# Linear attention, then a top-1 mixture of experts: narrower expert passes, one store fewer at the end, the later decays made earlier, and the stores of places one at a time

## The chip, the cores and the metric

The kernel runs on one core of a Trainium2 chip. The metric is the device time of one execution in microseconds (us), the median over the runs. Lower is better.

## The reference

Two blocks follow each other. Attention works on 4 batches of 8 heads, 768 positions and head size 64, all in fp32, with a decay `lam[h]` per head. In steps of 64 positions (the kernel takes 128):

```python
intra = einsum('bhij,bhjd->bhid', einsum('bhic,bhjc->bhij', qb, kb) * Dmask, vb)  # Dmask[i,j] = lam**(i-j), i >= j
inter = einsum('bhid,bhde->bhie', qb * lam**(pos+1), kv_state)
out[block] = intra + inter
kv_state   = lam**block * kv_state + einsum('bhsd,bhse->bhde', kb * lam**(block-1-pos), vb)
```

The result is laid out as 3072 tokens of 512 numbers. Each token then goes to the one of 8 experts with the highest gate logit:

```python
logits = x @ w_gate                       # 512 -> 8
e      = argmax(logits);  gate = softmax(logits)[e]
out[t] = gate * (relu(x[t] @ w1[e]) @ w2[e])   # 512 -> 1024 -> 512
```

With the reference's own inputs experts 0 to 7 get 385, 361, 364, 401, 418, 380, 356 and 407 tokens.

## The kernel before

**Attention** runs in 12 steps: 6 stretches of 128 positions, each in two steps of two batches. One step turns q and k on TensorE (line 227), scales k for the state on GpSimd (`kd`, line 255), multiplies q with k (`sp`, line 265), applies the decay mask on VectorE (`mt`, line 271), multiplies with v (`op`, line 299), adds the part of the state (`op`, line 290), and makes the state's update (`cp`, line 324). The function `enter(i)` does the loads, the turns and `kd` of step i; it is called one step ahead. Most instructions are pinned with `pin`, so that an engine runs them in the order in which the code writes them. Each engine, and each DMA queue, is a queue in that order.

**Decays.** The mask `decay` and `kdec` are made at the start. `later_decays()` (line 967) makes two more tables on VectorE, `qdec` and `sdec`, by copies and four scans. They are first used in the steps of the second stretch, by `qs_room` (line 241) and `sd` (line 336). Before, they are made after the first step's state has been copied (line 344).

**Places.** When the experts of a group of tokens are known, `ranks` and `put` work out each token's place in its expert's list, and `store(j)` (line 449) writes 128 list entries of 16 bytes to DRAM with an indirect DMA on GpSimd's queue. There are 24 such stores. `store_places()` (line 1018) issues two or three of them back to back at the end of a step, with a small memset between two of them. After the group called `early` is stored, `start_early()` loads the first list of expert 5 and gathers its 256 rows (lines 475 and 505), so that this pass can begin while attention ends.

**Experts.** Expert 5 comes first, in a part of 256 and a part of 128 places. The other seven are sorted on the device by how many tokens they have, and pass i takes `CAPS[i]` places whatever expert it is; unused places hold a row of zeros. Each of these passes has two stages, x times w1 (line 706) and hidden times w2 (line 889), with 112 matmuls each: 7 products instead of 8 are made from halves of the operands, so a matmul is `CAPS[i]/2` columns wide. If a count is beyond its `CAPS[i]`, a loop at the end (after the branches on `beyond`, lines 1270 to 1279) takes the rest in blocks of 128 rows, with the weights loaded again.

**The last pass** (`outputs_fast`, line 810 and after) makes its second stage in tiles of 128 rows. Rows 0 to 255 are made as four quarters. Its inner function `give(i, k, p)` finishes the quarter of row tile i and column half k and stores it at once, as half rows (`scatter_half`, line 527). Rows from 256 on are a tile of their own (`lone_tile`, stored by line 511).

Of the kernel before, what the change touches and what calls it, by code (L numbers as in the profile page):

```python
# [12 lines left out]
I32 = mybir.dt.int32  # L13
# [9 lines left out]
def kernel(  # L23
# [29 lines left out]
    nc = tc.nc  # L53
# [4 lines left out]
    P = 128  # L58
    C = P
    NSTEP = S // C  # L60
# [2 lines left out]
    FC = F // P  # L63

    FIRST = 5
    CAPS = [384, 424, 408, 408, 392, 368, 368, 360]
    TG = 3
    NR = E - 1

# [96 lines left out]
            data1=ident, initial=0.0, op0=ALU.mult, op1=ALU.add)  # L166

    kdec = const.tile([P, H], F32, name="kdec")
    nc.vector.tensor_copy(kdec.rearrange("p (g u) -> p u g", u=2), decay[:, :, :, C - 1])

    so_far = [const.tile([P, E], BF16, name="none_yet")]
    nc.vector.memset(so_far[0], 0.0)
# [45 lines left out]
    def pin(inst):  # L218
        tc.keep_in_program_order(inst)
# [89 lines left out]
    def to_sbuf(m):  # L309
        m.xT = work.tile([P, DC, 2, C], F32, tag="xT", name="xT", bufs=1)  # L310
        first = nc.scalar.copy(m.xT[:, :, 0, :], m.op[0])  # L311
        if swapped(m):
            with tc.issue_after(first.ins):
                nc.scalar.copy(m.xT[:, :, 1, :], m.op[1])
        else:
            for u in range(2):
                nc.scalar.copy(m.xT[halves[u], :, 1, :], m.op[1][halves[1 - u]])

    def grow(m):

# [196 lines left out]

    def half_rows(m):

        m.halves = small.tile([P, 2, 2], I32, tag="half_ids", name="half_ids", bufs=1)  # L520
        for k in range(2):
            pin(nc.vector.tensor_scalar(out=m.halves[:, :, k], in0=m.ids[:, :2, 1], scalar1=2,
                                        scalar2=k, op0=ALU.mult, op1=ALU.add))

    def scatter_half(idx, src):

        put = nc.gpsimd.indirect_dma_start(
            out=out.rearrange("n (k d) -> (n k) d", k=2),
            out_offset=bass.IndirectOffsetOnAxis(ap=idx, axis=0), in_=src,
            in_offset=None, bounds_check=2 * N - 1, oob_is_err=False)  # L530
        tc.declare_no_dep(put.ins, group="rows", reason="a token is on one list, once")
        tc.add_to_no_dep_group("rows", put.ins)
        return put
# [290 lines left out]
    def outputs_fast(m, w2t, b):  # L824
        a, t = left_of(m.hT, 0, P, pair_rooms_of_sums()), m.third
        o, outs, (p1, u2, u3, u4) = pair_rooms()
        add = nc.vector.tensor_add

        def scaled(i, k, u):
            nc.scalar.activation(outs[i][k], u, ACT.Copy, scale=at(m, i)[2])  # L830

        def give(i, k, p):
            pin(nc.vector.scalar_tensor_tensor(
                out=outs[i][k], in0=p, scalar=at(m, i)[2], in1=outs[i][k],
                op0=ALU.mult, op1=ALU.add))
            scatter_half(m.halves[:, i, k:k + 1], outs[i][k])

        half_rows(m)
        a.s3_made()
        t.s3_made()  # L840
        nc.scalar.copy(p1, block(a.a11, b.b11, 7))
        scaled(0, 0, p1)
        outputs(m, w2t, range(3, len(m.widths)), iter([4]))
        give(0, 0, block(a.a12, b.b21, 0))
        for make in (t.s1_made, t.s2_made, t.s4_made, a.s1_made, a.s2_made, a.s4_made):
            make()
        scaled(1, 0, block(a.a22, b.t4, 1))
        p3 = block(a.s3, b.t3, 5)
        lone_tile(m, 2, b, (4, 7, 0, 1))
        pin(add(u2, block(a.s2, b.t2, 4), p1))  # L850
        pin(add(u3, p3, u2))
        scaled(1, 1, u3)
        give(1, 0, u3)
        p5 = block(a.s1, b.t1, 7)
        give(1, 1, p5)
        pin(add(u4, p5, u2))
        scaled(0, 1, u4)
        give(0, 1, block(a.s4, b.b22, 0))
# [134 lines left out]
    lgs = {}  # L993
    base = [ebase]

    def enter(i, between=nothing):
        load(i + 1, "v") if i == 0 else nothing()
        load(i + 2, "qk")
        load(i + 1, "v")
        if i + 3 == len(steps):  # L1000
            load(i + 2, "v")
        n, b = steps[i]
        m = SimpleNamespace(n=n, b=b, qT=[], qsT=[], kT=[], kd=[], mt=[])
        m.q, m.k, m.v = (loaded[i, name] for name in "qkv")
        for s, turn_one in ((0, turn_q), (0, turn_k), (1, turn_q), (1, turn_k)):
            turn_one(m, s)
            between()
            between = nothing
        for s in range(2 if i == 0 else 0):
            score(m, s)  # L1010
        return m
# [3 lines left out]
    waiting = []  # L1015
    between = const.tile([P, 1], F32, name="between")

    def store_places(pin=pin):
        def some(group, i):
            return min(i + (3 if group[0] == NSTEP - 4 else 2), len(group[1]))  # L1020

        for group, store, i in waiting:
            for j in range(i, some(group, i)):
                if j > i:

                    pin(nc.gpsimd.memset(between, 0.0))
                pin(store(j))
        done = [group for group, _, i in waiting if some(group, i) == len(group[1])]
        waiting[:] = [(group, store, some(group, i)) for group, store, i in waiting
                      if some(group, i) < len(group[1])]  # L1030
        if any(group[:2] == early for group in done):
            start_early()

    def give_places(group):

        waiting.append((group, put(*group), 0))

    def give_ranks():
        return [ranks(*chosen.pop())] if chosen else []
# [38 lines left out]
    def start_early():  # L1078

        nc.vector.tensor_scalar(out=skip, in0=had, scalar1=-1.0, scalar2=float(EARLY),  # L1080
                                op0=ALU.mult, op1=ALU.add)
        nc.vector.tensor_scalar_max(skip, skip, 0.0)
        base[0] = const.tile([P, E], F32, name="ebase_late")
        nc.vector.tensor_copy(base[0], ebase)
        nc.vector.tensor_add(base[0][:, FIRST:FIRST + 1], base[0][:, FIRST:FIRST + 1], skip)
        w1t = wpool.tile([P, DC, F], F32, tag="w1", name="w1t")
        w2t = wpool.tile([P, FC, MD], F32, tag="w2", name="w2t")
        parts = [slice(0, DC // 2), slice(DC // 2, DC)]

        def load_half(p):  # L1090
            pin(nc.sync.dma_start(out=w1t[:, p], in_=w1_r[FIRST][:, p]))

        m = make_pass(FIRST, 0, EARLY, "0a", pin, nc.gpsimd)
        for p in parts:
            load_half(p)
        begun = fetch(m, 1 + (NSTEP - 2) * B * C, pin)
        behind = nc.sync.dma_start(out=w2t, in_=w2_r[FIRST])
        pin(behind)
        for other in begun:
            tc.add_manual_dep(behind.ins, other.ins.name, mybir.DependencyInfo(  # L1100
                mybir.DependencyClass.Sync, mybir.DependencyReason.DATA),
                reason="the gathers have the DMA engines first")
        weights.append((w1t, w2t))
        passes.append(m)

    cur, last = enter(0), None
    pin(nc.scalar.dma_start(out=gates[0][:, :, :E],
                            in_=moe_w_gate.rearrange("(c p) e -> p c e", p=P)))
# [2 lines left out]
    for i in range(len(steps)):  # L1111
        rest = leave(last, (4, 6, 7) if i < len(steps) - 1 else (4, 2, 3)) if last else nothing

        if i == 1:
            grow(cur)
        ahead = enter(i + 1, rest) if 0 < i < len(steps) - 1 else None
        if ahead:
            if last:
                with tc.issue_after(ahead.copied.ins):
                    store_rows(last)  # L1120
        else:
            rest()
            if last:
                store_rows(last)
        attend_begin(cur)
        if cur.n < NSTEP - 1:
            attend_states(cur)
            if i != 1:
                grow(cur)
            attend(cur)  # L1130
        else:
            attend(cur)
            if ahead:
                for s in range(2):
                    score(ahead, s)
            attend_states(cur)
        to_sbuf(cur)
        if i == 0:
            ahead = enter(1)
        update(cur)  # L1140
        if i == 0:
            later_decays()

        score_now = ahead and cur.n < NSTEP - 1
        if score_now:
            score(ahead, 0)
        ranked = give_ranks()
        if score_now:
            score(ahead, 1)
        for group in ranked:  # L1150
            give_places(group)
        if 0 < i < 3:
            empty_lists(i - 1)
        if ahead:
            fade(ahead)
            store_places()
        if i == len(steps) - 2:
            turn(passes[0], pin)
        last, cur = cur, ahead
    leave(last)()  # L1160
    store_rows(last)
    store_places(lambda inst: inst)
    give_places(*give_ranks())
    store_places(lambda inst: inst)


    cnt = bank(7, [P, E], "cnt")
# [149 lines left out]
```

## Time and profile before

| | us |
|---|---|
| median of 3 runs | 445.44 |
| the runs | 442.97, 445.44, 445.73 |
| the profiled execution, its time | 445.75 |
| its span, first to last instruction | 444.0 |

The profiled execution lies 0.31 us above the median. Its span has three parts: attention (to about 137 us, with the early pass inside it from 125 us on), the seven sorted passes (177 to 418 us, with one stage behind the other), and the last pass's second stage with the stores of its rows (to 444 us).

### The profile page before, as it was taken

Reading aid. Unit: us, or ns where it says so; the run is one execution under the profiler, and the core shown is the slowest. Engines: PE = TensorE matmul, PEld = TensorE weight load, DVE = VectorE, ACT = ScalarE, POOL = GpSimd, SP = SyncE. Lnnn points to the kernel's source line nnn. Section 1 sums busy time; section 2 is a strip of 40 time slices with the busy share of each in tenths; the row PEclk is TensorE's granted clock in tenths of the full one; section 3 lists DMA queues with packets and bytes.
Section 4 is the critical chain, followed back from the end, with each engine's and each line's share of the span. In section 5 each row is a group of like instructions: output and inputs, shape, how many; then the busy total and the mean of one; then the engine's idle time right before and its main releaser. Section 6 shows DMA issues by size and latency. Waiting matters only on the chain.

```text
span 444.0 us, 9564 instructions
## 1 busy us (share of the span) xinstructions
PE 425.9 (96%) x3687; PEld 396.6 (89%) x3687; DVE 270.6 (61%) x589; ACT 175.9 (40%) x315; POOL 256.9 (58%) x205
## 2 busy tenths in 40 slices
PE   5899999899999999999999999999999999999993
PEld 3788888788878897999999999999999999999972
DVE  2857566766558646567557656765565665775462
ACT  3266554444542224723354164334504615332221
POOL 4243645463323556667948675693876778649024
PEclk9999999999989999999999999999999999999998
DMA  9999989999681956969157947765974894853112
GB/s 175 208 246 255 226 210 205 249 213 261 229 239 53 296 123 176 321 173 347 27 100 154 387 87 165 272 205 88 276 277 79 172 371 105 155 183 49 27 68 73
DMA packets 164231, 83.48 MB, mean 188 GB/s; under 512 B 145515, under 2 KB 145559, under 8 KB 164176
## 3 DMA queue, kind: packets, MB, share of 16 engines
q1 hardware_dynamic: 155024, 63.21, 59.4%
q0 software_dynamic: 5216, 13.25, 9.8%
q10 hardware_dynamic: 3936, 6.31, 3.9%
q8 instruction: 31, 0.51, 0.5%
q14 instruction: 24, 0.20, 0.2%
HBM read 58.96 MB, written 13.16 MB: 162 GB/s over the span
## 4 chain that ended last, share of the span: by engine, by line
PE 86%; issue 4%; SPq 2%; ACT 2%; DVE 2%; DMA 1%; POOL 1%; POOLq 0%; ACTq 0%
PE p L706 29%; PE p L889 25%; PE sp L265 6%; PE op L299 5%; PE ph L584 3%; PE cp L324 3%; PE tx L360 3%; PE p L752 3%; PE op L290 3%; PE tk L227 2%; PE tq L227 2%; PE lgT L350 2%; SPq L555 1%; DMA k_in<-in_k_dram 1%; SPq L105 1%
## 5 line engine op out<-in xcount | busy, mean ns | idle before, releaser
L511 POOL DMA_INDIRECT out_dram<-o_room,list x23 | 23.4, 1016 | 46.5 <-ACT o_room L932 23.7
L271 DVE TENSOR_TENSOR mt<-sp,decay 128x512 f32<-128x512 f32 x48 | 30.6, 685 | 27.1 <-PE sp L265 22.5
L449 POOL DMA_INDIRECT slots<-entry,slot_i x24 | 23.5, 979 | 34.6 <-DVE slot_i L447 17.1
L717 ACT ACTIVATE hT<-hT 128x408 f32<-128x408 f32 (+4 forms) x56 | 28.4, 523 | 34.3 <-DVE hT L714 30.8
L706 PE MATMUL p<-xgT,w1t 128*128 128x204 f32 (+4 forms) x224 | 41.9, 329 | 0.0
L706 PEld LDWEIGHTS p<-xgT,w1t 128*128 128x128 f32 x224 | 37.5, 190 | 0.8 <-issue 0.8
L255 POOL TENSOR_TENSOR kd<-k_in,kdec 128x512 f32<-128x512 f32 x20 | 20.6, 1048 | 29.3 <-PE cp L324 14.5
L596 ACT COPY u_qT<-p 128x408 f32<-128x408 f32 (+4 forms) x14 | 6.8, 482 | 72.2 <-PE p L706 72.2
L889 PE MATMUL p<-hT,w2t 128*128 128x204 f32 (+3 forms) x192 | 34.0, 330 | 0.0
L889 PEld LDWEIGHTS p<-hT,w2t 128*128 128x128 f32 x192 | 32.3, 190 | 0.0
L265 PE MATMUL sp<-qT,kT 64*128 64x128 f32 x384 | 28.6, 295 | 1.6 <-DVE qT L235 1.3
L505 POOL DMA_INDIRECT xg<-xs,list x25 | 25.8, 1034 | 6.7 <-issue 6.0
L265 PEld LDWEIGHTS sp<-qT,kT 64*128 64x128 f32 x384 | 24.7, 199 | 4.5 <-issue 2.8
L714 DVE TENSOR_TENSOR hT<-p,u_kd 128x408 f32<-128x408 f32 (+4 forms) x28 | 15.8, 564 | 20.8 <-PE p L706 20.0
L633 POOL TENSOR_TENSOR s_q<-w1t 128x1024 f32<-128x1024 f32 x7 | 16.5, 2360 | 20.5 <-DVE t_xT L691 15.9
L311 ACT COPY xT<-op 128x512 f32<-128x512 f32 x12 | 7.0, 586 | 42.0 <-PE op L299 33.1
L299 PE MATMUL op<-mt,v_in 128*64 128x128 f32 x384 | 23.5, 273 | 0.0
L584 PE MATMUL ph<-xgT,w1t 128*128 128x256 f32 (+1 forms) x128 | 21.9, 329 | 0.0
L299 PEld LDWEIGHTS op<-mt,v_in 128*64 128x64 f32 x384 | 21.0, 137 | 0.5 <-ACT kT L249 0.3
L706 PE MATMUL p<-t_sd,w1t 128*128 128x204 f32 (+4 forms) x112 | 20.9, 329 | 0.0
L706 PE MATMUL p<-st,s_q 128*128 128x204 f32 (+4 forms) x112 | 20.9, 329 | 0.0
L706 PE MATMUL p<-xgT,s_v 128*128 128x204 f32 (+4 forms) x112 | 20.8, 328 | 0.0
(239 smaller groups left out, 1087.7 us busy)
## 6 DMA issues: line engine op xcount, KB each, us to landing
w2t<-in_moe_w_dram SPq DMA_DIRECT2D x8, 2048.0 KB
w1t<-in_moe_w_dram SPq DMA_DIRECT2D x7, 2048.0 KB
v_in<-in_v_dram SPq DMA_DIRECT2D x12, 512.0 KB
xs<-x_room ACTq DMA_DIRECT2D x12, 512.0 KB
q_in<-in_q_dram SPq DMA_DIRECT2D x11, 512.0 KB
k_in<-in_k_dram SPq DMA_DIRECT2D x11, 512.0 KB
o_room<-qs_room SPq DMA_DIRECT2D x76, 48.0 KB
w1t<-in_moe_w_dram SPq DMA_DIRECT2D x2, 1024.0 KB
```

Of the source, the lines that this page charges most:

```text
L227: pin(nc.tensor.transpose(t[:, i, b, :], src[:, b, h:h + 2, :], ident))
L255: pin(nc.gpsimd.tensor_tensor(out=kd, in0=m.k[:, :, hs], in1=kdec[:, hs].unsqueeze(1).unsqueeze(3).to_broadcast(shp), op=ALU.mult))
L265: pin(nc.tensor.matmul(sp[u][:, i, b, :], lhsT=m.kT[s][halves[u], i, b, :], rhs=m.qT[s][halves[u], i, b, :], start=(i == 0 and b == 0), st ...
L271: nc.vector.tensor_mul(mt[:, u], sp[u], decay[:, u, s * HP // 2:(s + 1) * HP // 2].unsqueeze(2).to_broadcast(shp))
L299: pin(nc.tensor.matmul(out_at(m, b, u, hp), lhsT=m.v[:, b, 2 * hp + u, :], rhs=m.mt[hp // 2][:, u, hp % 2, b, :], start=(first and hp == 0 ...
L449: put = nc.gpsimd.indirect_dma_start(out=slots, out_offset=bass.IndirectOffsetOnAxis(ap=slot_i[:, i:i + 1], axis=0), in_=entry[:, n, bs[i] ...
L505: return nc.gpsimd.indirect_dma_start(out=dst, out_offset=None, in_=xs[:rows, :], in_offset=bass.IndirectOffsetOnAxis(ap=idx, axis=0))
L511: put = nc.gpsimd.indirect_dma_start(out=out, out_offset=bass.IndirectOffsetOnAxis(ap=idx, axis=0), in_=src, in_offset=None, bounds_check= ...
L584: nc.tensor.matmul(ph, lhsT=w1t[:, dc, fc * P:(fc + 1) * P], rhs=m.xgT[:, dc, :], start=(dc == 0), stop=(dc == DC - 1))
L706: nc.tensor.matmul(p[:, i, :], lhsT=lhs[:, dc, g, i * P:(i + 1) * P], rhs=rhs[:, dc, :], start=(dc == 0), stop=(dc == DH - 1))
L717: pin(nc.scalar.activation(outs[i][k], outs[i][k], ACT.Relu))
L889: nc.tensor.matmul(p[:, c, :], lhsT=lhs[:, f, c * P:(c + 1) * P], rhs=rhs[:, f, :], start=(f == 0), stop=(f == FC // 2 - 1))
```

## The change

It has four parts. `CAPS` is given in multiples of 4 instead of 8. Row tile 1 of the last pass is stored once, with whole rows, when its second half is done. `later_decays()` is called before the first step, tied behind `kdec`. And the stores of places are handed out one by one: in most steps one at the step's end and one inside `enter` between the two `kd`; after the early gathers one store follows at once, and the next waits until the step's output has been copied (`copied`).

```diff
-    CAPS = [384, 424, 408, 408, 392, 368, 368, 360]
+    CAPS = [384, 420, 408, 404, 388, 364, 364, 356]
...
-        m.halves = small.tile([P, 2, 2], I32, tag="half_ids", name="half_ids", bufs=1)
+        m.halves = small.tile([P, 2], I32, tag="half_ids", name="half_ids", bufs=1)
...
-            scatter_half(m.halves[:, i, k:k + 1], outs[i][k])
+            if i == 0:
+                scatter_half(m.halves[:, k:k + 1], outs[i][k])
+            elif k == 1:
+                scatter(at(m, i)[1], o[i])
...
+            if (s, turn_one) == (0, turn_k):
+                store()
...
+    def store_places(most, pin=pin):
+        put = None
+        for k in range(min(most, len(waiting))):
+            group, store, j = waiting.pop(0)
+            if k > 0:
+                pin(nc.gpsimd.memset(between, 0.0))
+            put = store(j)
+            pin(put)
+            if group[:2] == early and j == 1:
+                start_early()
+        return put
...
+    with tc.issue_after(keys_made.ins):
+        later_decays()
     cur, last = enter(0), None
...
+        spread = i < len(steps) - 3
+        ahead = (enter(i + 1, rest, (lambda: store_places(1)) if spread else nothing)
+                 if 0 < i < len(steps) - 1 else None)
...
+        copied = to_sbuf(cur)
+        if i == len(steps) - 2:
+            tc.add_manual_dep(store_places(1).ins, copied.ins.name, mybir.DependencyInfo(
+                mybir.DependencyClass.Sync, mybir.DependencyReason.DATA),
+                reason="the gathers have the queue alone")
...
-        if i == 0:
-            later_decays()
...
-            store_places()
+            store_places(1 if i < 6 or i == len(steps) - 3 else 2)
```

On VectorE, at the start of attention (`decay` and `kdec` are the first tables, `mt` the masked products of the first step):

```order
 L169 COPY kdec<-decay 128x2x4
-L271 TENSOR_TENSOR mt<-sp_207,decay 128x512
-L271 TENSOR_TENSOR mt<-sp_208,decay 128x512
-L271 TENSOR_TENSOR mt<-sp_220,decay 128x512
-L271 TENSOR_TENSOR mt<-sp_221,decay 128x512
-L344 COPY st<-cp 128x512
-L970 COPY lam_pair<-lam_bc 64x4 x2
-L972 SCALAR_TENSOR_TENSOR qdec<-lam_pair,zeros 128x128 x4
-L975 COPY sdec<-qdec 128x4
+L974 COPY lam_pair<-lam_bc 64x4 x2
+L976 SCALAR_TENSOR_TENSOR qdec<-lam_pair,zeros 128x128 x4
+L979 COPY sdec<-qdec 128x4
```

The seven instructions of the later decays stood between the state's copy and `qT`; now they stand ahead of the first mask.

On GpSimd, in steps 6 and 7 of attention (`slots` are the lists in DRAM, `between` the memset), before:

```order
L449 DMA slots<-entry,slot_i 27648x4
L1026 MEMSET between 128x1
L449 DMA slots<-entry,slot_i 27648x4
L1026 MEMSET between 128x1
L449 DMA slots<-entry,slot_i 27648x4
L255 TENSOR_TENSOR kd<-k_in,kdec 128x512 x2
L336 TENSOR_TENSOR sd<-st,sdec 128x512
L449 DMA slots<-entry,slot_i 27648x4 x2
```

and with the change:

```order
L450 DMA slots<-entry,slot_i 27648x4
L1030 MEMSET between 128x1
L450 DMA slots<-entry,slot_i 27648x4
L255 TENSOR_TENSOR kd<-k_in,kdec 128x512
L450 DMA slots<-entry,slot_i 27648x4
L255 TENSOR_TENSOR kd<-k_in,kdec 128x512
L337 TENSOR_TENSOR sd<-st,sdec 128x512
L450 DMA slots<-entry,slot_i 27648x4
```

Three stores in a row have become two, and the third stands between the two `kd`, behind the first one's wait.

On GpSimd at the kernel's end (the last two lists are those of the last two passes), before:

```order
L511 DMA out_dram<-o_room,list_2434 3072x512 x3
L527 DMA out_dram<-o_room,half_ids 6144x256
L511 DMA out_dram<-o_room,list_2446 3072x512
L527 DMA out_dram<-o_room,half_ids 6144x256 x3
L1270 TENSOR_LOAD beyond
L1271 COMPARE_AND_BRANCH
```

and with the change:

```order
L512 DMA out_dram<-o_room,list_2428 3072x512 x3
L528 DMA out_dram<-o_room,half_ids 6144x256
L512 DMA out_dram<-o_room,list_2440 3072x512 x2
L528 DMA out_dram<-o_room,half_ids 6144x256
L1279 TENSOR_LOAD beyond
L1280 COMPARE_AND_BRANCH
```

Behind the lone tile's store there are two stores where there were three.

## Rows read from the trace of the kernel before

**Rows 1.** The page, sections 1 and 2: TensorE, and the DMA engines' mean rate.

```profile
PE 425.9 (96%) x3687; PEld 396.6 (89%) x3687; DVE 270.6 (61%) x589; ACT 175.9 (40%) x315; POOL 256.9 (58%) x205
...
DMA packets 164231, 83.48 MB, mean 188 GB/s; under 512 B 145515, under 2 KB 145559, under 8 KB 164176
```

**Rows 2.** The chain of waits, three stages of the passes: start, us, what.

```profile
196.27 20.07 PE p L889 x112
216.34 19.32 PE p L706 x112
...
400.58 17.08 PE p L706 x112
```

**Rows 3.** Timeline of VectorE at the start: start, us, instruction, idle before and its releaser.

```profile
11.63 1.29 DVE L271 TENSOR_TENSOR mt<-sp,decay 128x512 f32<-128x512 f32 x2 [5.26 <-PE sp L265]
...
15.49 0.33 DVE L970 COPY lam_pair<-lam_bc 64x4 f32<-64x4 f32 x2
15.86 2.97 DVE L972 TENSOR_TENSOR_SCAN qdec<-lam_pair,zeros 128x128 f32<-128x128 f32 x4
...
18.94 1.29 DVE L235 COPY qT<-tq 128x512 f32<-128x512 f32 x2
```

**Rows 4.** Timeline of ScalarE, same place: the copies of the turned keys.

```profile
18.21 1.07 ACT L249 COPY kT<-tk 128x512 f32<-128x512 f32 x2
```

**Rows 5.** Timeline of TensorE, same place.

```profile
19.78 2.06 PE L265 MATMUL sp<-qT,kT 64*128 64x128 f32 x32 [1.30 <-DVE qT L235]
```

**Rows 6.** Timeline of GpSimd in attention: a pair of `kd`, and stores of places.

```profile
56.19 2.03 POOL L255 TENSOR_TENSOR kd<-k_in,kdec 128x512 f32<-128x512 f32 x2 [2.43 <-issue]
...
83.72 1.01 POOL L449 DMA_INDIRECT slots<-entry,slot_i  x1 [4.24 <-DVE slot_i L447]
...
86.30 0.96 POOL L449 DMA_INDIRECT slots<-entry,slot_i  x1 [0.19 <-issue]
...
121.60 0.97 POOL L449 DMA_INDIRECT slots<-entry,slot_i  x1 [0.18 <-issue]
```

**Rows 7.** Timeline of TensorE in attention: idle times that no wait ends.

```profile
65.78 0.98 PE L324 MATMUL cp<-v_in,kd 128*64 128x64 f32 x26 [0.17 <-issue]
...
86.54 0.26 PE L324 MATMUL cp<-v_in,kd 128*64 128x64 f32 x1 [0.31 <-issue]
87.28 0.34 PE L324 MATMUL cp<-v_in,kd 128*64 128x64 f32 x3 [0.48 <-issue]
88.01 0.94 PE L324 MATMUL cp<-v_in,kd 128*64 128x64 f32 x24 [0.40 <-issue]
...
122.01 0.47 PE L290 MATMUL op<-qs_room,st 64*64 64x128 f32 x5 [0.67 <-issue]
123.47 1.62 PE L290 MATMUL op<-qs_room,st 64*64 64x128 f32 x24 [0.99 <-issue]
```

**Rows 8.** Busy time by stretch: length, the five engines, clock, DMA share, GB/s.

```profile
121.00:123.50 2.50, 0.84 (x9) 0.59 (x11) 0.00 (x0) 0.00 (x0) 1.38 (x3) 1.00 0.46 159
123.50:127.00 3.50, 3.50 (x37) 3.17 (x37) 3.22 (x6) 1.15 (x3) 0.00 (x0) 0.52 0.76 88
```

**Rows 9.** Line 1097, a load behind the early gathers: duration min/median/max, first and last start.

```profile
L1097 SPq DMA_DIRECT2D w2t<-in_moe_w_dram x1: 368/368/368, 123.1 to 123.1; - x1
```

**Rows 10.** Timeline of GpSimd at the end: the last three stores.

```profile
436.20 1.00 POOL L527 DMA_INDIRECT out_dram<-o_room,half_ids  x1 [0.31 <-issue]
437.51 0.97 POOL L527 DMA_INDIRECT out_dram<-o_room,half_ids  x1 [0.30 <-DVE o_room L833]
438.78 0.97 POOL L527 DMA_INDIRECT out_dram<-o_room,half_ids  x1 [0.30 <-issue]
```

**Rows 11.** Timeline of VectorE at the end: its last instruction.

```profile
436.69 0.48 DVE L833 SCALAR_TENSOR_TENSOR o_room<-p,list,o_room 128x256 f32<-128x256 f32 x1 [0.87 <-PE p L752]
```

**Rows 12.** Line 1271, the branch past the loop: duration, first and last start.

```profile
L1271 POOLq EVENT_SEMAPHORE  x5: 17/43/43, 441.2 to 441.5; - x5
...
L1271 POOLq COMPARE_BRANCH  x1: 62/62/62, 437.8 to 437.8; - x1
```

More of the change, by code (lines that the diff above doesn't have):

```diff
@@ L168 @@
     kdec = const.tile([P, H], F32, name="kdec")
-    nc.vector.tensor_copy(kdec.rearrange("p (g u) -> p u g", u=2), decay[:, :, :, C - 1])
+    keys_made = nc.vector.tensor_copy(kdec.rearrange("p (g u) -> p u g", u=2), decay[:, :, :, C - 1])
     so_far = [const.tile([P, E], BF16, name="none_yet")]
@@ L317, in to_sbuf @@
                 nc.scalar.copy(m.xT[halves[u], :, 1, :], m.op[1][halves[1 - u]])
+        return first
     def grow(m):
@@ L518, in half_rows @@
     def half_rows(m):
-        m.halves = small.tile([P, 2, 2], I32, tag="half_ids", name="half_ids", bufs=1)
+        m.halves = small.tile([P, 2], I32, tag="half_ids", name="half_ids", bufs=1)
         for k in range(2):
-            pin(nc.vector.tensor_scalar(out=m.halves[:, :, k], in0=m.ids[:, :2, 1], scalar1=2,
+            pin(nc.vector.tensor_scalar(out=m.halves[:, k:k + 1], in0=m.ids[:, 0, 1:2], scalar1=2,
                                         scalar2=k, op0=ALU.mult, op1=ALU.add))
@@ L994, with enter @@
     base = [ebase]
-    def enter(i, between=nothing):
+    def enter(i, between=nothing, store=nothing):
         load(i + 1, "v") if i == 0 else nothing()
@@ L1016 @@
     between = const.tile([P, 1], F32, name="between")
[L1018 to L1032, printed above, removed]
+    def store_places(most, pin=pin):
[9 more added lines that the diff above has]
+        return put
     def give_places(group):
-        waiting.append((group, put(*group), 0))
+        store = put(*group)
+        waiting.extend((group, store, j) for j in range(len(group[1])))
     def give_ranks():
@@ L1115 @@
             grow(cur)
-        ahead = enter(i + 1, rest) if 0 < i < len(steps) - 1 else None
+        spread = i < len(steps) - 3
+        ahead = (enter(i + 1, rest, (lambda: store_places(1)) if spread else nothing)
+                 if 0 < i < len(steps) - 1 else None)
         if ahead:
@@ L1136 @@
             attend_states(cur)
-        to_sbuf(cur)
+        copied = to_sbuf(cur)
[3 more added lines that the diff above has]
+                reason="the gathers have the queue alone")
         if i == 0:
@@ L1161 @@
     store_rows(last)
-    store_places(lambda inst: inst)
+    store_places(len(waiting), lambda inst: inst)
     give_places(*give_ranks())
-    store_places(lambda inst: inst)
+    store_places(len(waiting), lambda inst: inst)
     cnt = bank(7, [P, E], "cnt")
```

## The prediction

> **What bounds the kernel now.** I read the page's first two sections first [rows 1]: TensorE is busy for 96% of the span, so work moved between the other engines counts only where TensorE waits for it. The reader is to see two things there: only what shortens TensorE's own work, or one of its few idle times, can move the end; and VectorE, ScalarE and GpSimd have room. Then the chain of waits, which tells what that work is: from 177 to 418 us the stages of the sorted passes stand one behind the other, 112 matmuls each [rows 2], and a stage's time follows its width. Third, the timelines of the start [rows 3 to 5], where TensorE waits 1.30 us for `qT`, and of attention, where I looked for idle times that no wait ends [rows 7] and laid GpSimd's stores beside them [rows 6]. Last the end, where GpSimd's stores and the branch behind them follow the last arithmetic [rows 10 to 12].
>
> **Narrower passes.** The width 424 took 20.07 us, 408 took 19.32 and 360 took 17.08 [rows 2]. From the first and the last, 2.99 us for 64 places are 0.0467 us a place (408 lies on that line to 0.01 us). Five passes lose 4 places in both stages, and the last pass loses 4 in its first stage alone, since its second is in tiles of fixed size: 11 stages x 4 x 0.0467 = **-2.06 us**, all on TensorE's path. What no row shows is a matmul of half a width such as 210, 202 or 178, which isn't a multiple of 4 as 212, 204 and 180 are. If such a matmul takes the time of the next multiple of 4, the term is 0; a gain beyond 2.06 us is excluded by the line. I take -2.06, the value of the line on which three shown widths lie. GpSimd, VectorE and ScalarE also do a little less there, which counts nothing.
>
> **Decays made early.** Seven instructions leave the time between the state's copy and `qT`. They ran from 15.49 us to the start of `qT` at 18.94 [rows 3], 3.45 us. They now stand ahead of the first `mt`, where VectorE idled 5.26 us before 11.63 while it waited for `sp` [rows 3]; that holds them with 1.8 us to spare, so I cost the new place at nothing. Were that cover gone, the first step would start up to 3.45 us late. `qT` can then be done before `kT`: the two copies on ScalarE start at 18.21 and take 1.07 together [rows 4], half of it for the first, which ends at 18.75 and is next late. TensorE starts `sp` at 19.78 [rows 5], 0.20 us after the first `qT` by the same halving (18.94 + 0.645 [rows 3]); 0.20 us after 18.75 it would start at 18.95: **-0.83 us**. The bounds are 0 and the whole wait, -1.30.
>
> **Three stores at the end.** Row tile 1 costs one store where it cost two. The stores now start at 436.20, 437.51 and 438.78 [rows 10]. VectorE's last result is there at 436.69 + 0.48 = 437.17 [rows 11], so the last of three still starts at about 437.5, and 1.27 us of GpSimd's work go. But GpSimd has its branch at 437.8, ahead of the end of its last store, and its next event at 441.2 to 441.5 [rows 12]; 3.4 us lie between them, and the end follows the later one. As the branch can't come before the last result, I take only **-0.05 us**; the bounds are 0 (the branch ends last) and -1.27 (the store does). The page "Runtime: NRT & Kernel Launch" of the Trainium skill (section Instruction fetch mechanics) says that a taken branch out of the window of instructions held has to fetch its target first. By it the branch ends last and the term is 0 to -0.05, which rows 12 bear out with 3.4 us; no row here shows a fetch by name.
>
> **Stores spread.** Every store remains, so GpSimd saves nothing. One now stands between two `kd`, which alone can cost: the second `kd` comes one store and its gap later, 0.96 + 0.30 us [rows 6, 10]. The pair that ended at 58.22 [rows 6] is used by the `cp` at 65.78 [rows 7], 7.5 us later, so I cost this at nothing; with that cover gone it would be 1.3 us in each of some ten steps. Where a store waits for the step's copied output, only further stores stand behind it on GpSimd, and no `kd`.
>
> What may be gained are TensorE's idle times without a releaser. They grow with what GpSimd issues in a row: 0.17 us at an ordinary pair; 0.31 + 0.48 + 0.40 = 1.19 us at the three stores from 83.72 to 87.26; 0.67 + 0.99 = 1.66 us at two gathers and two stores, the last at 121.60 [rows 6, 7]. There the granted clock falls too, from 1.00 to 0.52, that is from 2.4 to 1.2 GHz, for the 3.50 us after TensorE had stood for most of 2.5 us [rows 8]; at full speed that work would take 3.50 x 0.52 = 1.82 us, so this costs 1.68 us more. The change shortens the three to two, and the second group by its last store. That the stores cause these times is inferred from where they fall. I take half of what the triple costs above a pair, (1.19 - 0.17)/2 = **-0.5 us**, and nothing of the second group, whose two gathers and first store stay. The bounds are +0.5 (the idle times are only handed to other steps) and -1.19 - 1.66 - 1.68 = -4.53.
>
> A rule of the Trainium skill speaks against this term: by the same page and section, a sequencer fetches its instructions in blocks with a DMA queue of its own. By it the idle times would be late blocks, come at the same places of the program whatever GpSimd stores, and the term would be 0. The trace speaks for it in that they are not waits, and against it in that the DMA engines were only 0.46 busy while TensorE stood [rows 8]; no row shows a fetch late. It is the second case below.
>
> **The sum.** -2.06 - 0.83 - 0.05 - 0.5 = -3.44. The profiled execution took 445.75 us, so 442.31; it lies 0.31 above the median of the three runs, which gives **442.0 us**, 0.8% less. About 1% is what a measurement of this kernel can tell from no change.
>
> **The cases.**
> 1. The forecast, 442.0, with the terms' own spread about 441 to 443.3: **0.33**.
> 2. The idle times don't hang on the stores: -2.94, so **442.5**. For it: nothing shows the cause. Against: their size follows the bursts [rows 6, 7]. **0.22**.
> 3. The stop at 121 us and its half clock go. Line 1097's load, which waits for the early gathers, starts at 123.1 [rows 9], 0.4 us before TensorE runs on; so the stop lasts while the burst is being worked off, and a burst with one store less may fall short of what stops it. It gives -2.94 - 1.66 - 1.68 = -6.28, so **439.2**. The runs speak for it: one took 442.97 and the others 445.44 and 445.73, a difference of such a size as this stop would make if it came in some executions only. Against: two gathers and a store are still in a row. **0.27**.
> 4. Half widths that aren't multiples of 4 run no faster: -1.38, so 444.4 - 0.31 = **444.1**. For it only that no row shows one. **0.09**.
> 5. Slower: a list overflows. The counts in order are 418, 407, 401, 385, 364, 361, 356 against 420, 408, 404, 388, 364, 364, 356 places: two lists are exactly full, and the first one starts with 384 for 380. One token more in a full list, where a logit on the chip is rounded the other way, and the loop at the end runs. It would load an expert's 4 MB at 188 GB/s [rows 1], 22.3 us; compute 128 rows, by the stages at 408 2 x 19.32 x 128/408 x 8/7 = 13.9 us (8 products there, not 7); and take branches of 3.4 us twice: +43, so **485**. It decides at one token above 364 or 356. Against: the counts are those of inputs that don't change. **0.03**.
> 6. The stores between the `kd` make `cp` late in some steps, by 1.3 us each, and eat up the gain: **444 to 448**, 0.06.
>
> **Range and chances.** 438.6 to 444.8 us takes in cases 1 to 4 with their bounds and leaves out case 5, half of case 6 and tails of case 3. Faster by over 1% is below 440.99: case 3 but for its upper tail (0.25) and case 1's lower tail (0.05), so 0.30. Slower by over 1%, above 449.9: case 5 and a little of case 6, 0.04. The rest, 0.66, is within 1%.
>
> **What the profile after would show.** The stages' rows in the chain: 19.88 us at 420 and 16.89 at 356 if the widths pay, 20.07 and 17.08 if not. The first `mt` at 11.63 still, `qT` some 3 us earlier, and 18.95 for TensorE's `sp` at 19.78. The last store at about 437.5 and the branch's next event still near 441.2. The idle times marked "issue" at three stores fall to about 0.2 to 0.7 us; near 121 us the clock at 0.52 for some 3.5 us in case 1, at 1.00 throughout in case 3. I am wrong if `cp` waits for `kd` anywhere, if new idle times come up where a single store now stands, or if the loop at the end runs.

## The result: 439.8 us against 445.6 us, of which a second comparison bears out 1.4 to 2.0 us

The changed kernel took 439.79 us (median of four runs, 438.43 to 440.71), the kernel before in the same comparison 445.59 (442.97 to 446.1): a ratio of 0.9894 (95% interval 0.9849 to 0.9939). That lies inside the forecast's range, 2.2 us below its value, outside the 441 to 443.3 us of its first case, and just inside what it called faster, to which it gave 0.30.

The experiments below ran on three chips, the kernel before on all three and the changed kernel again on one of them. The kernel before took 440.89 us there (median of 97 runs, 437.23 to 443.88), and the changed kernel 438.99 us beside 441.00 on the same chip, 2.0 us less; the ratio of the comparison is **0.9969 (0.9942 to 0.9997)**, 1.4 us or 0.3%. Executions in a slower state are left out of medians and ratios: two in experiment 3 (446.11 and 2460.55 us), one each in experiments 4 (444.78) and 8 (869.49), and one of the kernel before (444.10). A ratio here is the comparison's own estimate and not the quotient of two medians, which can lie up to 0.4% away from it.

The changed kernel thus took about the same in both comparisons; three of the first four runs of the kernel before took longer than any of the 97 later ones. Some 4 us of the first difference hang on those runs. Whether the change took this time away, or it would have gone without it, as in all later runs, the first comparison can't tell.

Where the time lies was read by the start of TensorE's k-th matmul, which can be counted in every profile of both kernels (3687 each). First the two profiles of the first comparison, then two from one later chip:

| stretch (matmuls) | before | changed | difference | before, later chip | changed, later chip | difference |
|---|---|---|---|---|---|---|
| start to 440 | 39.42 | 38.47 | -0.95 | 38.15 | 37.95 | -0.20 |
| 440 to 1600, attention | 73.29 | 69.16 | **-4.13** | 68.21 | 68.21 | **0.00** |
| 1600 to 1800, early gathers | 17.47 | 16.79 | -0.68 | 18.54 | 18.85 | +0.31 |
| 1800 to 2100 | 42.06 | 42.06 | 0.00 | 42.05 | 42.06 | +0.01 |
| 2100 to 3600, sorted passes | 249.72 | 247.88 | **-1.84** | 249.74 | 247.87 | **-1.87** |
| 3600 to the end of the span | 21.99 | 21.98 | -0.01 | 21.97 | 21.43 | -0.54 |
| span | 444.0 | 436.3 | -7.7 | 438.7 | 436.4 | -2.3 |

### The profile page after: what moved, and what is told of

The parts are those of the page before. It is cut to its first block, busy times and chain, and to the rows that moved or that the text cites. A ratio compares the mean times of both kernels' runs of the same rounds, so it can differ in the third digit from the quotient of the medians.

```text
span 436.3 us, 9559 instructions
## 1 busy us (share of the span) xinstructions
PE 419.9 (96%) x3687; PEld 391.9 (90%) x3687; DVE 264.9 (61%) x589; ACT 175.5 (40%) x315; POOL 255.1 (58%) x198
## 4 chain that ended last, share of the span: by engine, by line
PE 82%; issue 6%; SPq 3%; DMA 3%; DVE 2%; POOL 2%; ACT 1%; POOLq 0%; DVEq 0%; ACTq 0%
PE p L707 28%; PE p L893 26%; PE ph L585 5%; PE p L753 4%; PE sp L265 3%; PE op L299 3%; SPq L107 2%; PE tx L361 2%; DMA k_in<-in_k_dram 2%; PE op L290 2%; PE tk L227 2%; PE cp L325 2%; PE tq L227 2%; PE p L761 1%; PE lgT L351 1%
## 5 line engine op out<-in xcount | busy, mean ns | idle before, releaser
L718 ACT ACTIVATE hT<-hT 128x364 f32<-128x364 f32 (+5 forms) x56 | 28.3, 521 | 34.4 <-DVE hT L715 29.7
L707 PE MATMUL p<-xgT,w1t 128*128 128x182 f32 (+5 forms) x224 | 41.5, 327 | 0.0
L597 ACT COPY u_qT<-p 128x364 f32<-128x364 f32 (+5 forms) x14 | 6.7, 479 | 71.7 <-PE p L707 71.7
L893 PE MATMUL p<-hT,w2t 128*128 128x182 f32 (+4 forms) x192 | 33.7, 329 | 0.0
L715 DVE TENSOR_TENSOR hT<-p,u_kd 128x364 f32<-128x364 f32 (+5 forms) x28 | 15.7, 561 | 21.0 <-PE p L707 20.2
L707 PE MATMUL p<-t_sd,w1t 128*128 128x182 f32 (+5 forms) x112 | 20.7, 327 | 0.1
L707 PE MATMUL p<-st,s_q 128*128 128x182 f32 (+5 forms) x112 | 20.7, 327 | 0.0
L707 PE MATMUL p<-t_xT,w1t 128*128 128x182 f32 (+5 forms) x112 | 20.6, 326 | 0.0
```

Source lines behind the costliest of these rows:

```text
L707: nc.tensor.matmul(p[:, i, :], lhsT=lhs[:, dc, g, i * P:(i + 1) * P], rhs=rhs[:, dc, :], start=(dc == 0), stop=(dc == DH - 1))
L718: pin(nc.scalar.activation(outs[i][k], outs[i][k], ACT.Relu))
L893: nc.tensor.matmul(p[:, c, :], lhsT=lhs[:, f, c * P:(c + 1) * P], rhs=rhs[:, f, :], start=(f == 0), stop=(f == FC // 2 - 1))
```

## The profile after

The chain of waits, stages of the passes (start, us, what), answers to [rows 2]:

```profile
190.34 19.90 PE p L893 x112
210.24 19.32 PE p L707 x112
...
248.88 19.16 PE p L707 x112
...
393.14 16.91 PE p L707 x112
```

424 became 420 and 20.07 became 19.90; the stage at 408 is still 19.32; at 404 it is 19.16; 360 became 356 and 17.08 became 16.91. Halves of 210, 202 and 178 columns pay for what they save, 0.16 to 0.17 us a stage.

VectorE at the start (start, us, instruction, idle before and its releaser), answers to [rows 3]:

```profile
6.63 2.89 DVE L976 TENSOR_TENSOR_SCAN qdec<-lam_pair,zeros 128x128 f32<-128x128 f32 x4
...
11.11 1.29 DVE L271 TENSOR_TENSOR mt<-sp,decay 128x512 f32<-128x512 f32 x2 [1.38 <-PE sp L265]
```

TensorE, same place, answers to [rows 5]:

```profile
17.96 2.06 PE L265 MATMUL sp<-qT,kT 64*128 64x128 f32 x32 [0.35 <-ACT kT L249]
...
24.53 0.63 PE L227 MATMUL tk<-ident,k_in 128*128 128x128 f32 x4 [0.68 <-DMA k_in<-in_k_dram]
```

The decays are hidden, with 1.38 us of VectorE's idle time left ahead of `mt`. `sp` waits for `kT` now, as forecast. But 6 us later a new row stands: TensorE waits 0.68 us for a load of `k`, which the first profile of the kernel before doesn't have there.

TensorE in attention, the idle times that no wait ends, answers to [rows 7]; these two are all between 60 and 105 us:

```profile
83.38 0.99 PE L325 MATMUL cp<-v_in,kd 128*64 128x64 f32 x26 [0.20 <-issue]
...
103.32 0.99 PE L325 MATMUL cp<-v_in,kd 128*64 128x64 f32 x26 [0.15 <-issue]
```

GpSimd's last stores ahead of these two:

```profile
81.87 0.96 POOL L450 DMA_INDIRECT slots<-entry,slot_i  x1 [0.19 <-issue]
...
101.80 0.95 POOL L450 DMA_INDIRECT slots<-entry,slot_i  x1 [0.19 <-issue]
```

Each idle time begins 0.35 to 0.42 us after the store has ended.

TensorE behind the early gathers, where [rows 7] had a stop without a releaser:

```profile
118.96 0.30 PE L571 MATMUL tp<-ident,xg 128*128 128x128 f32 x1 [1.86 <-DMA xg<-xs,list_0a]
120.32 0.98 PE L571 MATMUL tp<-ident,xg 128*128 128x128 f32 x7 [1.06 <-DMA xg<-xs,list_0a]
```

No stop stands in `op` (line 291) any more. In its place there is a wait with a name: the first product with the gathered rows waits 1.86 us for the first gather, and the next ones 1.06 us more for the second. By stretch (length, the five engines, clock, DMA share, GB/s), answers to [rows 8]:

```profile
121.00:123.50 2.50, 2.50 (x35) 1.83 (x35) 1.41 (x6) 1.97 (x5) 1.55 (x2) 1.00 0.75 212
123.50:127.00 3.50, 3.50 (x70) 3.08 (x66) 1.62 (x11) 1.06 (x4) 1.31 (x5) 1.00 1.04 341
```

The clock stayed at 1.00 in this execution. The end, VectorE's last instruction, answers to [rows 11]:

```profile
429.07 0.48 DVE L834 SCALAR_TENSOR_TENSOR o_room<-p,list,o_room 128x256 f32<-128x256 f32 x1 [0.87 <-PE p L753]
```

GpSimd's last two stores, answers to [rows 10]:

```profile
428.57 1.00 POOL L512 DMA_INDIRECT out_dram<-o_room,list  x1 [0.30 <-DVE x_room L860]
429.87 0.98 POOL L528 DMA_INDIRECT out_dram<-o_room,half_ids  x1 [0.30 <-DVE o_room L834]
```

And the branch behind them (duration, first and last start), answers to [rows 12]:

```profile
L1280 POOLq EVENT_SEMAPHORE  x5: 17/43/43, 434.0 to 434.4; - x5
...
L1280 POOLq COMPARE_BRANCH  x1: 62/62/62, 430.2 to 430.2; - x1
```

The branch at 430.2 comes 0.65 us after VectorE's last result at 429.55, and the next event 3.8 us later.

## The experiments

Experiments 1 to 4 take the parts one by one. Two causes were held against each other for the idle times that are missing in the changed kernel: fewer stores in a row, or the earlier start, which shifts attention against its loads. From experiment 5 on Theory A says that the widths pay and the rest is nearly nothing, and Theory B that the four parts add up as in the first comparison, because bursts of stores stop TensorE. Ratios are to the kernel before, run on the same chip beside each; between experiments on different chips (1 to 4 and 9 to 11 on one, 5 to 8 on a second, 12 on a third) ratios are compared and not times alone.

**1. The widths alone.**

```diff
-    CAPS = [384, 424, 408, 408, 392, 368, 368, 360]
+    CAPS = [384, 420, 408, 404, 388, 364, 364, 356]
```

Expected: 

> The kernel before with the narrower passes alone. In the profile of the change the stages at 420, 404, 364 and 356 took about 0.17 us less each than those at 424, 408, 368 and 360, 11 stages: both theories (the stores' bursts made TensorE's idle times; or the earlier start shifted attention against the loads and the idle times went with that) expect -1.85 us, so a ratio of 0.996, attention as before, with the idle times at the three stores and behind the early gathers as they were.

Measured: 439.40 us, 0.9971 (0.9935 to 1.0006). The interval takes in the size and also no change; the profile shows the size, 247.85 us from the 2100th to the 3600th matmul where experiment 6 took 249.73. What did not fit is that the idle times at the bursts were missing, though the stores stood as before: the 440th to the 1600th matmul took 68.21 us.

**2. The early decays alone.**

```diff
+    with tc.issue_after(keys_made.ins):
+        later_decays()
     cur, last = enter(0), None
...
-        if i == 0:
-            later_decays()
```

Expected: 

> The kernel before with the early decays alone. If the stores' bursts make TensorE's idle times: the start gains some 0.9 to 1.3 us, part of which a load of k takes back near 24 us, and the idle times at the bursts stay, so about -0.9 us (0.998). If instead the shift of attention against the loads made them go: idle times of some 3.6 us between 39 and 115 us vanish here too, so about -4.5 us (0.990).

Measured: 440.97 us, 1.0014 (0.9978 to 1.005). The -4.5 us of an earlier start are excluded; a gain of 0.9 us is just inside the interval. TensorE at the start:

```profile
16.19 0.63 PE L227 MATMUL tk<-ident,k_in 128*128 128x128 f32 x4 [1.04 <-DMA k_in<-in_k_dram]
...
17.62 2.06 PE L265 MATMUL sp<-qT,kT 64*128 64x128 f32 x32
...
24.58 0.63 PE L227 MATMUL tk<-ident,k_in 128*128 128x128 f32 x4 [1.07 <-DMA k_in<-in_k_dram]
```

`sp` waits for nothing here, but the turns of `k` wait for two loads, 1.04 and 1.07 us. In this execution the start is bound by the loads: what is saved between them is waited for at the next one, and the 440th matmul starts at 38.52 us, 0.4 us later than in experiment 6 with the old decays.

**3. The spread stores alone.** The kernel before with the change's `store_places`, its store between the two `kd`, and the store that waits for `copied`; the core:

```diff
-        ahead = enter(i + 1, rest) if 0 < i < len(steps) - 1 else None
+        spread = i < len(steps) - 3
+        ahead = (enter(i + 1, rest, (lambda: store_places(1)) if spread else nothing)
+                 if 0 < i < len(steps) - 1 else None)
```

Expected: 

> The kernel before with the stores of places spread alone (and the store behind the early gathers held until the output is copied). If the bursts make the idle times: some 3.6 us between 39 and 115 us vanish, and near 121 us a wait for the early gathers of some 3 us takes the place of the stop and its half clock, so about -4 us (0.991). If the earlier start did it: about 0 to -1 us, with idle times as before.

Measured: 441.27 us, 1.0025 (0.9988 to 1.0061). No gain; the -4 us of the bursts lie outside the interval.

**4. Three stores at the end alone.**

```diff
-            scatter_half(m.halves[:, i, k:k + 1], outs[i][k])
+            if i == 0:
+                scatter_half(m.halves[:, k:k + 1], outs[i][k])
+            elif k == 1:
+                scatter(at(m, i)[1], o[i])
```

Expected: 

> The kernel before with three stores at the end alone. If GpSimd's branch ends last, as the prediction took it: -0.05 us, the last store starting near 437.5 and the branch's next event still 3.4 us behind the branch. If the last store's landing ends it: -1.27 us. The idle times in attention as in the kernel before by either theory.

Measured: 440.20 us, 0.9991 (0.9956 to 1.0026). From the last matmul's start to the end of the span the profiles took 7.0 to 8.1 us with four stores (seven of them) and 6.9 to 7.7 with three (seven); the means, 7.6 and 7.4, differ by less than either scatters. A gain of 1.27 isn't seen; one of 0.05 can't be seen.

**5. The changed kernel again**, unchanged.

Expected: 

> The changed kernel itself, again. Theory A (of the four parts only the widths pay in every execution; TensorE's idle times at the bursts, in the first profile of the kernel before, belonged to that execution and not to the stores, since they were missing with the old bursts in three of the last four kernels): -1.85 us, a ratio of about 0.996. Theory B (the four parts add up as they did in the first comparison): 0.987 to 0.990.

Measured: 438.99 us, 0.9969 (0.9942 to 0.9997). Theory A's 0.996 lies inside, Theory B's 0.987 to 0.990 outside.

**6. The kernel before, unchanged**, for a profile of the same chip.

Expected: 

> The kernel before, unchanged, for a profile from the same chip. Theory A: from the 440th to the 1600th matmul it takes 68.2 us, as the last four kernels did, with no idle time at the three stores, where the first profile took 73.3. Theory B: the idle times at the three stores and behind the early gathers are there again, 73 us.

Measured: 441.63 us. GpSimd's three stores in a row are there:

```profile
80.21 1.01 POOL L449 DMA_INDIRECT slots<-entry,slot_i  x1 [3.77 <-DVE slot_i L447]
81.22 0.11 POOL L1026 MEMSET between<- 128x1 f32 x1
81.52 0.96 POOL L449 DMA_INDIRECT slots<-entry,slot_i  x1 [0.19 <-issue]
82.48 0.11 POOL L1026 MEMSET between<- 128x1 f32 x1
82.78 0.96 POOL L449 DMA_INDIRECT slots<-entry,slot_i  x1 [0.19 <-issue]
```

and TensorE at the same time runs its `cp` in one piece:

```profile
81.73 0.72 PE L290 MATMUL op<-qs_room,st 64*64 64x128 f32 x19
82.38 1.15 PE L324 MATMUL cp<-v_in,kd 128*64 128x64 f32 x32
83.36 1.92 PE L299 MATMUL op<-mt,v_in 128*64 128x128 f32 x32
```

In [rows 7] the same `cp` was cut into four pieces by 1.19 us of idle time. And near 118 us stands the wait that the changed kernel has too:

```profile
118.08 0.30 PE L570 MATMUL tp<-ident,xg 128*128 128x128 f32 x1 [2.25 <-DMA xg<-xs,list_0a]
119.41 0.98 PE L570 MATMUL tp<-ident,xg 128*128 128x128 f32 x7 [1.03 <-DMA xg<-xs,list_0a]
```

By stretch:

```profile
40.00:110.00 70.00, 70.00 (x1175) 61.97 (x1176) 45.83 (x139) 40.20 (x85) 35.64 (x43) 1.00 1.04 231
115.00:120.50 5.50, 2.22 (x40) 1.79 (x31) 1.76 (x4) 1.22 (x4) 3.48 (x5) 1.00 0.53 135
120.50:124.00 3.50, 3.50 (x33) 2.56 (x33) 1.33 (x8) 2.02 (x5) 2.14 (x4) 0.52 0.89 157
```

TensorE is busy for all of the 70 us of attention, then for 2.22 of 5.50 us while it waits for the gathers, and the clock is 0.52 for the 3.5 us after that.

**7. The turns of the early rows later**, on the changed kernel, to test that wait.

```diff
                 store_rows(last)
+        if i == len(steps) - 1:
+            turn(passes[0], pin)
         attend_begin(cur)
...
-        if i == len(steps) - 2:
-            turn(passes[0], pin)
```

Expected: 

> The changed kernel with the turns of the early rows put behind the logits of the step before the last, so that TensorE has about 2.3 us of other work while the early gathers land. If the wait for these gathers and the half clock behind it are what is left to gain near 116 to 125 us: the wait of 2.9 us falls to about 0.6 and the half clock goes in most executions, 2.3 to 4 us less than the changed kernel (0.986 to 0.991 of the kernel before, if that one is at 0.996), and the times scatter less. If the gathers' landing sets the pace in any case (the products of the early pass need the rows): the wait only moves to these products, 0 to -1 us.

Measured: 435.93 us, 0.992 (0.9887 to 0.9954), 3.1 us under the changed kernel's 438.99 beside it. The wait was real time: from the 1600th to the 1800th matmul 14.96 us where experiment 5 took 18.85. The times did not scatter less, as was expected: 434.57 to 440.28, five of twelve above 437, where experiment 5 had 437.64 to 441.30.

**8. The same move on the kernel before.** The same edit.

Expected: 

> The kernel before with the same move of the turns of the early rows, nothing else. If that wait is the same in both kernels: -2.3 to -4 us (0.991 to 0.995). If the changed stores alone make it: 0.

Measured: 437.45 us, 0.9946 (0.9913 to 0.998). So the wait is in both kernels, and neither burst nor spread makes it.

**9. The turns in the middle of the last step's products with v**, on the changed kernel.

```diff
-    def attend(m):
+    def attend(m, between=nothing):
...
+            if (hp, b, u) == (HP // 2 - 1, 1, 1):
+                between()
...
-            attend(cur)
+            attend(cur, (lambda: turn(passes[0], pin)) if i == len(steps) - 1 else nothing)
```

Expected: 

> The changed kernel with the turns of the early rows in the middle of the last step's products with v, some 0.95 us of TensorE's work later than in the last run but one that moved them (where 0.79 us of wait for the second gather was left). If that wait is the rest of what can be had there: 0.7 us less than that run, 0.990 of the kernel before. If the products of the early pass now wait for the turned rows instead: no better than it, 0.992 or above.

Measured: 434.73 us, **0.9848** (0.9798 to 0.9898), and five executions within 434.42 to 435.24. TensorE at the place:

```profile
116.21 0.66 PE L363 MATMUL tx<-ident,xT 128*128 128x128 f32 x4 [0.54 <-ACT xT L313]
...
118.32 1.09 PE L299 MATMUL op<-mt,v_in 128*64 128x128 f32 x16
119.35 1.44 PE L573 MATMUL tp<-ident,xg 128*128 128x128 f32 x8
120.71 1.09 PE L299 MATMUL op<-mt,v_in 128*64 128x128 f32 x16
```

and by stretch:

```profile
115.00:120.50 5.50, 4.84 (x72) 3.52 (x65) 3.44 (x15) 2.97 (x8) 4.28 (x5) 1.00 0.71 237
120.50:124.00 3.50, 3.50 (x60) 2.84 (x59) 0.99 (x4) 1.68 (x4) 1.71 (x5) 1.00 0.81 128
```

Other work covers the gathers, TensorE is busy for 4.84 of the 5.50 us, and the clock stays at 1.00. The ratio lies 0.7% under experiment 7's, more than the 0.7 us expected, though the two intervals just overlap. At the place itself the two profiles differ by 0.07 us (14.96 and 14.89 us from the 1600th to the 1800th matmul; the wait left in experiment 7 was 0.51 us): what is missing here are the executions above 437 us.

**10. Every store of the first three stretches twice**, on the kernel before; the second goes to a list that nobody reads.

```diff
                 pin(store(j))
+                if group[0] <= NSTEP - 4:
+                    pin(store(j, spare))
```

Expected: 

> The kernel before with every store of places of the first three stretches issued twice, the second time to a list that nobody reads, so four stores in a row where there were two and six where there were three. If bursts make idle times on TensorE in every execution (theory B): more of those marked "issue", 0.5 us and more at each burst, 2 to 5 us in all, or waits of cp for a late kd. If they don't (theory A): no idle time at the bursts, the 440th to the 1600th matmul in 68.2 us as before, ratio 1.00.

Measured: 443.79 us, 1.0058 (1.0023 to 1.0093). GpSimd now issues six stores from 80.33 to 87.65 us; TensorE meanwhile:

```profile
82.33 1.15 PE L325 MATMUL cp<-v_in,kd 128*64 128x64 f32 x32
83.31 1.92 PE L300 MATMUL op<-mt,v_in 128*64 128x128 f32 x32
85.16 1.16 PE L266 MATMUL sp<-qT,kT 64*128 64x128 f32 x16
...
91.75 1.10 PE L291 MATMUL op<-qs_room,st 64*64 64x128 f32 x30 [0.26 <-DVE lg L377]
```

Nothing stops it during the burst. The 0.26 us at 91.75 is the only idle time above 0.1 us between 44 and 110 us, and it is a wait for VectorE; with the slower matmuls beside it, the 440th to the 1600th took 68.89 us and not 68.2. The rest of the 2.6 us is lost elsewhere, with 20.91 us from the 1600th to the 1800th matmul where experiment 6 took 18.54: the first early gather is waited for 3.45 us and the second 0.89, and the half clock lasts 6.8 us (120.4 to 127.2). That gathers land later when more stores went ahead is seen in this one profile only.

**11. Widths, three stores at the end and the later turns, but old decays and old stores of places**: the edits of 1, 4 and 7 on the kernel before.

Expected: 

> The kernel before with the narrower passes, the three stores at the end and the later turns of the early rows, but decays and stores of places as before. Against the same move of the turns on the changed kernel it differs by the decays and the stores of places alone. Theory A (neither gains anything): the same as that one, 0.991 to 0.993. Theory B (the stores spread save idle times): 1 to 4 us more, 0.995 to 1.001.

Measured: 435.98 us, 0.9899 (0.9845 to 0.9952), against 435.93 us and 0.992 in experiment 7. In the times Theory A holds. In its profile, though, the wait that the early decays were to shorten is there, 1.31 us for `qT`, as in [rows 5]:

```profile
19.67 2.06 PE L265 MATMUL sp<-qT,kT 64*128 64x128 f32 x32 [1.31 <-DVE qT L235]
```

**12. Experiment 9 with old decays and old stores of places**: the edits of 1, 4 and 9 on the kernel before.

Expected: 

> The fastest kernel so far (the changed kernel with the turns of the early rows in the middle of the last step's products with v: 434.73 us, five executions within 0.8 us) with decays and stores of places as in the kernel before. As the scatter near 121 us is gone there, what these two parts are worth can be seen to half a us. Theory A (nothing): 434.2 to 435.3 us. Theory B (the spread stores save idle times): 436 us or more, with idle times marked "issue" between 40 and 115 us. If the decays alone are worth their predicted 0.83 us: about 435.6.

Measured: 435.13 us, 0.9875 (0.9834 to 0.9916); five of the six executions took 434.42 to 435.42, the sixth 439.53. That lies in Theory A's range, but the comparison is weaker than hoped: experiments 9 and 12 are 0.4 us apart by their medians and 0.27%, or 1.2 us, by their ratios, each of which has an interval of 0.4 to 0.5% to either side. Their profiles reach the 1600th matmul at 106.21 and 106.41 us. No gain of the 0.83 + 0.5 in the forecast is seen, and the times alone don't exclude it.

## Why the prediction held, and which of its steps did not

**Narrower passes: right.** -2.06 was the term, -1.84 and -1.87 us are what the two pairs of profiles show. Each stage saves 0.16 to 0.17 us and not 0.187: from 420 to 356 it is 2.99 us again, so the slope held, and the new widths lie about 0.02 us a stage above the line. Case 4 (half widths without profit) is out.

**Decays: wrong, by its "next late".** The cover held, and `kT` was next. What failed is that the forecast looked no further than that wait. In the kernel before on the later chip `sp` waited only 0.33 us for `qT`, not 1.30 as in [rows 5], and the turns of `k` behind it waited 0.60 us for a load; with the decays early that load is waited for longer (experiment 2). What the term is worth hangs on the execution. Of the nine profiles with the old decays two have the wait of 1.3 us for `qT`, the first one and experiment 11; they start the 440th matmul at 39.42 and 39.31 us, and the other seven at 38.03 to 38.74. The five with early decays start it at 37.95 to 38.52. So the part saves about 1 us where that wait occurs and nothing that shows elsewhere; the -0.83 had been read from one execution. A part of the profiles' differences at the start is no effect of the change at all: the 32 `sp` of the first step took 3.79 us in both first profiles, 3.16 in experiment 6 and 2.74 in experiment 2, where the same 32 took 2.06 a step later; the first record of a full clock stands at 14.25, 12.94, 11.44 and 10.46 us in these four, and at 14.04 us in experiment 11: the two executions with the wait are those with the latest full clock of all fourteen.

**Stores at the end: right**, as far as can be seen. GpSimd's last store now starts 0.3 us after VectorE's last result, the branch comes 3.8 us ahead of the next event where it was 3.4, and the 1.27 us of GpSimd's work bought nothing that shows: from the last matmul's start to the end both first profiles took 7.75 us. The Trainium skill's page "Runtime: NRT & Kernel Launch" (section Instruction fetch mechanics) holds that a taken branch outside the instructions at hand waits for a fetch; the 3.8 us agree with it. Between 430.3 and 434.0 us the trace lists four packets of the instruction queues; whose they are, and that GpSimd waits for them, it doesn't show.

**Stores spread: the inference did not hold.** The term rested on idle times that grew with the bursts [rows 6, 7]. They stood in one profile. With the same bursts they were absent in experiments 1, 2, 4 and 6, and six stores in a row made none (10). Nor did `kd`'s cover fail: no `cp` waited for it. So the term is 0 in every later run, and the value of the forecast's second case was the right one for the stores.

**The total: inside the range by luck.** Of the sum of -3.44 only the widths are there in every run. The base it was taken from, 445.44, lies 4.4 us above the 441.00 that the kernel before took on the chip where both were run again; from there the sum would have given 437.6, and 438.99 was measured. What the first comparison showed beyond the widths, 4.13 us of it in attention, no term foresaw in that size. Its 439.79 lies nearest to case 3's 439.2, whose mechanism, as follows, gave nothing either.

**The stop at 121 us (case 3): half right.** There was time to be had at this place, but not by the stores. In the first profile TensorE came to the first product with gathered rows at 125.13 us, 6.1 us after the second gather was issued, and waited for nothing there; where it comes earlier it waits for the gathers by name, 2.25 + 1.03 us in experiment 6, and in the changed kernel 1.86 + 1.06. Case 3's sign, the clock at 1.00, stood in the changed kernel's first profile, and yet its 3.34 us were not gained: 16.79 us against 17.47, and 18.85 against 18.54 on the later chip. What made the stop in `op` isn't known. The gathers hang on a row of transfers: in experiment 6 the last store of places they need was issued at 100.95, the list's load waited for its landing until 108.38, and the first gather for the list until 114.43.

**Case 5** (a list overflows) did not occur, nor case 6.

**What stays open.** What made the idle times in the first profile of the kernel before isn't known. From the 440th to the 1600th matmul it took 5.1 us longer than later; 2.5 us of this are idle times, 2.0 of them ended by no wait, and the rest is longer spacing of the matmuls beside them. The changed kernel's first profile kept two of 0.15 and 0.20 us, and none of the later profiles of either kernel has them at the bursts. In both first profiles those that stand alone in `cp` begin 0.35 to 0.5 us after a store has ended; in the kernel before [rows 7]'s 65.78 comes behind

```profile
64.30 0.96 POOL L449 DMA_INDIRECT slots<-entry,slot_i  x1 [0.19 <-issue]
```

which ends 0.35 us before the idle time begins. One of 0.20 us in `sp`, at 80.43, has no store near it. So the stores may have had a part in them there, together with something that the later runs did not show, and the change may have saved time there. Whether it did could not be tried. Late blocks of instructions, the reason of the forecast's second case, are not shown either: from 85.0 to 88.9 us and from 121.0 to 123.5 us the first trace lists no packet of an instruction queue.

## What to carry to other kernels

An idle time that no wait ends is a fact of one execution until a second profile of the same kernel shows it; a term that rests on it should be held at 0 until then. When work is taken off a path early in a kernel that streams its inputs, look at the next load that is waited for, not only at the next engine. And a wait for a transfer costs twice where the clock falls after it: other work put into the wait (here a reordering of eight matmuls, 1.2 to 1.5% in all with the narrower passes) was worth more than the four parts of the change together in the later comparison, and in experiments 9 and 12 it took the scatter away in ten of eleven executions.

## What the runs showed of the hardware that was not expected

The scatter of this kernel has one main source. Of the 97 executions of the kernel before, the 32 with a mean granted clock of 0.994 or more have a median of 438.68 us, and the 34 with 0.988 or less 442.27. In the profiles the difference lies behind the early gathers: the clock was at half (1.2 GHz) for 3.41 us in experiment 6 after TensorE had stood for 2.25 + 1.03 us, for 6.83 us in experiment 2, and not at all in the first profile of the change after 1.86 + 1.06 us. Where other work filled the wait, ten of eleven executions (experiments 9 and 12) stayed at 0.996 to 0.997. The Trainium skill's page "TensorE: Matmul & The Clock Gate" (section HAM oscillation — how this bites in real kernels) describes such a fall of the clock after waits for transfers, and the rows agree; that a wait of nearly the same length once keeps the clock and once loses it for 3.4 or 6.8 us is what these runs add. Shorter waits than the one that kept it lost it too: experiment 1 stood 1.11 + 0.98 us and had the half clock for 3.42 us.
